# A gated mix of attention and feed-forward: both parts of an output tile in one PSUM bank for three of four query blocks, with the gate ratio folded into the softmax reciprocals

## The chip, the cores and the metric

The kernel runs on one core of one Trainium2 chip. The metric is the device time of one execution in microseconds (us). Engine names in the profile: PE is TensorE, PEld its weight loads, ACT is ScalarE, DVE is VectorE, POOL is GpSimd, SP is SyncE, whose queue issues most of the transfers.

## What is computed

For 2048 rows of width 512 the kernel computes attention with 32 heads of 16, a SwiGLU feed-forward part of width 1792, and a mix of both with one gate per row. All tensors are bf16.

```python
x = A_x
g = _sigmoid((x * gate_w).sum(-1, keepdims=True))
qkv = (x @ wqkv) ...                       # 32 heads of 16
p = _softmax(q @ k * 16 ** -0.5)           # 2048 keys
a = (p @ v) @ wo
b = (_silu(x @ w_gate) * (x @ w_up)) @ w_down
return g * a + (1 - g) * b
```

## The kernel before

**Units.** The queries are cut into four blocks of 512 (QB), the heads into eight groups of four (G). A unit is one block and one group: 32 units, ordered in UNIT (line 115): group 0 of all four blocks first, then groups 1 to 7 of block 0, of block 1, and so on. A unit has 16 key tiles of 128 keys, and each key tile four score blocks of 128x512, one for each head. A slot, the planner's clock, is one key tile: 512 slots.

**Two engines take exponentials.** PE writes the scores of two heads into one tile s_t of 128x1024 (emit_pair, line 715), of which there are two; ACT turns it into e_t (line 727). A key tile done so costs two ACT instructions. Other key tiles go to DVE (emit_d, line 748): PE writes each head's scores into a bank d_t, DVE evicts it to y_t with a scale that makes bf16 bits of an exponential, and once four are there, five more DVE operations on 128x2048 (z_t, u_t, two products, a last scale) improve them. Of these, the addition of the correction is an accumulating transfer on POOL's queue (line 795) or, near the end of the kernel, a DVE operation (add_here, line 786). v_unit (line 1368) decides when a tile goes to DVE: if by the planner's costs DVE would be done with it LEAD (16 us), or in the last unit LAST (11 us), before ACT is done.

**Weighted sums.** Four 32-column matmuls per key tile accumulate into one bank o_ps (pv, line 866). At the end of a unit DVE copies it to osb (post, line 903), and transfers on SP's queue put the head rows into onc and the denominators into a DRAM row dd (put, line 897).

**Softmax denominators.** At the end of a block, recip (line 928) loads the denominators back as 128x128 (dn), takes reciprocals on DVE (rn), stores them (rr), and loads them 16-fold as rows (rb). norm (line 944) multiplies onc by rb. The last two groups of the last block do this on chip (recip_here, and the end of the program).

**Feed-forward part.** For each block, 14 steps (gu_chain, line 650) make gate and up products of 128 of the 1792 columns in two banks gu; ACT takes a tanh (th), DVE makes gs and mt. The weights wg and wu come with w_load (line 642) on SP's queue, two steps ahead (line 1190). down_pieces (line 676) then multiplies mt by wd_t: 14 pieces of four 32-column matmuls into one bank dps for each of the four 128-row tiles of a block; DVE evicts it times the share 1 - g (omg) into bblk, or times ge = (1 - g) / g for the last block.

**Output.** For blocks 0 to 2, fin_pieces (line 997) multiplies onc by wo_t, four pieces into a bank a_ps; store (line 956) makes a_ps * g + bblk in one DVE operation and stores it. In the last block bblk is added by a matmul with ident (last_rows, line 966; last_pieces, tail), and the end of the program multiplies by g (lines 1503 to 1512).

**Gate.** gate_pieces and gate_end (lines 612 to 636): logits, clamped to -60 and 60, ge = exp(-logit), gval = 1 / (1 + ge) = g, omg = ge * gval = 1 - g.

**What sets the order.** The order of instructions on each engine is fixed when the program is built (ordered, line 146). A planner with a cost for each piece of PE, ACT and DVE work (spend, later, fill_dve) fills the gaps beside the scores. Side work is in chains with a release slot and a deadline (Pacer, line 48; lines 1170 to 1215); a chain that needs a bank takes one of three (m_tile, line 346), which it gives back when DVE has evicted it. The feed-forward part runs from slot 72 to slot 504, in the order of the blocks:

```python
FS = [(qb, fc) for qb in range(QB) for fc in range(FC)]                       # line 639
f0, f1 = 72, SLOTS - 8                                                        # line 1176
per = (f1 - f0) / QB
```

SP's queue issues its transfers in order, and a transfer that waits holds up those behind it. DRAM tiles such as dd and rr are in HBM.

Of the kernel before, what the change touches and what calls it, by code (L numbers as in the profile page):

```python
# [9 lines left out]
ALU = mybir.AluOpType  # L10
AX = mybir.AxisListType
BF16 = mybir.dt.bfloat16
F32 = mybir.dt.float32
# [66 lines left out]
def kernel(  # L80
# [13 lines left out]
    P = 128  # L94
    x = A_x.flatten_outer_dims()
    S, D = x.shape
    F = B_w_gate.shape[1]
    DH = 16
    H = D // DH
    G = H // 4  # L100
    NB = H // 8
    DC = D // P
    FC = F // P
    KT = S // P
    QBW = 512
    QB = S // QBW
    TQ = QBW // P
    assert H * DH == D and D % P == 0 and F % P == 0 and S % QBW == 0 and G == 8 and TQ == 4
    out_f = out.flatten_outer_dims()
# [3 lines left out]
    SLOTS = UNITS * KT  # L113
# [167 lines left out]
    gval = const.tile([P, KT], F32, name="gval")  # L281
    omg = const.tile([P, KT], F32, name="omg")
    ge = const.tile([P, KT], F32, name="ge")
    bblk = big.tile([P, TQ, D], BF16, name="bblk")


# [20 lines left out]
    def later(cost, f, ready=None, key=None):  # L307

        c = plan.chain
        if c is not None:  # L310
            c.owed += 1
        ready = plan.pe + 0.25 if ready is None else ready
        owed.insert(sum(o[0] <= ready for o in owed), (ready, cost, f, c, key))
# [101 lines left out]
    def columns(n, name, lhs, rhs, end, c0=0):  # L415

        st = {}

        def pc(k):
            def f():  # L420
                if k == 0:
                    st["p"] = m_tile(name)
                w, r = lhs(k), rhs(k)
                for j in range(4):
                    mm(st["p"][32 * j:32 * j + 32, c0:QBW], lhsT=w[:, 32 * j:32 * j + 32], rhs=r, start=(k == 0),
                       stop=(k == n - 1), tile_position=(0, 32 * j), skip_group_check=True)
                spend("C", 1)
                if k == n - 1:
                    end(st["p"])
            return f  # L430
        return [(1, pc(k), k == 0) for k in range(n)]
# [180 lines left out]
    def gate_pieces(t0):  # L612
        def f():
            gp = m_tile("glog")
            for t in (t0, t0 + 1):
                for dc in range(DC):
                    mm(gp[:, t:t + 1], lhsT=xT[:, dc, t * P:(t + 1) * P],
                       rhs=gw_col[:, dc:dc + 1], start=(dc == 0), stop=(dc == DC - 1))
            spend("F", 2)

            def end():
                vec.tensor_scalar(out=ge[:, t0:t0 + 2], in0=gp[:, t0:t0 + 2], scalar1=-60.0, scalar2=60.0,
                                  op0=ALU.max, op1=ALU.min)
                m_free(gp, plan.dve)
            later(0.15, end)
        return [(0.7, f, True, "F", None)]

    def gate_end():
        act(out=ge[:, :], in_=ge[:, :], func=ACT.Exp, scale=-1.0)
        plan.act += 0.2  # L630

        def end():
            vec.tensor_scalar(out=omg[:, :], in0=ge[:, :], scalar1=1.0, scalar2=None, op0=ALU.add)
            vec.reciprocal(gval[:, :], omg[:, :])
            vec.tensor_tensor(out=omg[:, :], in0=ge[:, :], in1=gval[:, :], op=ALU.mult)
        later(0.5, end, plan.act + 0.2)


    FS = [(qb, fc) for qb in range(QB) for fc in range(FC)]
    w_gate, w_up, gs_of = {}, {}, {}  # L640

    def w_load(i, gate):
# [33 lines left out]
    def down_pieces(qb, tq):  # L676

        def end(p):
            t, n = tq, qb * TQ + tq
            share = omg if qb < QB - 1 else ge  # L680
            vec.tensor_scalar(out=bblk[:, t, :], in0=p[:, 0:D], scalar1=share[:, n:n + 1],
                              scalar2=None, op0=ALU.mult)
            if qb == QB - 1:
                scaled.add(t)
            m_free(p, plan.dve)
        return columns(FC, "dps", lambda fc: mt[:, fc, tq * P:(tq + 1) * P], lambda fc: wd_t[:, fc, :],
                       lambda p: later(0.65, lambda: end(p)))
# [236 lines left out]
    def recip16(o, i):  # L924
        with nc.allow_low_precision(reason="bf16 reciprocal of softmax denominators is plenty accurate here"):
            vec.reciprocal(o, i)

    def recip(qb, g1, n0):

        n = 4 * g1  # L930
        dn = work.tile([P, P], BF16, tag="dn", name="dn")
        queue.dma_start(out=dn[0:4 * n, :], in_=dds[qb][0:n, :].rearrange("h (a c) -> (h a) c", c=P))

        def spread():
            rn = work.tile([P, P], BF16, tag="rn", name="rn")
            recip16(rn[0:4 * n, :], dn[0:4 * n, :])
            rr = dram.tile([H, QBW], BF16, tag="rr", name="rr")
            queue.dma_start(out=rr[0:n, :].rearrange("h (a c) -> (h a) c", c=P), in_=rn[0:4 * n, :])
            for b in range(g1 // 2):
                queue.dma_start(out=rb[:, b, :],  # L940
                                  in_=rr[8 * b:8 * b + 8, :].unsqueeze(1).broadcast_to([8, DH, QBW]))
        at.setdefault(n0 + 6, []).append(lambda: later(0.87, spread))
        for b in range(g1 // 2):
            def norm(b=b):
                vec.tensor_tensor(out=onc[qb][:, b, :], in0=onc[qb][:, b, :], in1=rb[:, b, :], op=ALU.mult)
                normed.add((qb, b))
            at.setdefault(n0 + 13 + b, []).append(lambda norm=norm: later(0.345, norm))

    def recip_here(osb):
# [2 lines left out]
        mm(dps[:, :], lhsT=sbc_t[:, :], rhs=osb[:, :], start=True, stop=True)  # L952
        rd = work.tile([P, QBW], BF16, tag="rd", name="rd")
        return dps, rd

    def store(t, a_ps, base, o_t=None):
        if o_t is None:
            o_t = opool.tile([P, D], BF16, tag="ot", name="o_t")[:, :]
        vec.scalar_tensor_tensor(out=o_t, in0=a_ps[:, 0:D], scalar=gval[:, t:t + 1], in1=base,
                                 op0=ALU.mult, op1=ALU.add)  # L960
        queue.dma_start(out=out_f[t * P:(t + 1) * P, :], in_=o_t)

    here_done = []
    a_ps = []
# [6 lines left out]
    def last_pieces():  # L971

        def keep(pa, pb):
            a_ps.extend([pa, pb])
        return two_banks(NB + 1, "a_l", last_rows(0), last_rows(1), keep, stop=False)
# [18 lines left out]
            w, r = last_rows(tq)(i)  # L994
            mm(a_ps[tq][:, 0:D], lhsT=w, rhs=r, start=(i == 0), stop=False)

    def fin_pieces(qb, tq):

        def end(p):
            store(qb * TQ + tq, p, bblk[:, tq, :])  # L1000
            m_free(p, plan.dve)
        return columns(NB, "a_ps", lambda b: onc[qb][:, b, tq * P:(tq + 1) * P], lambda b: wo_t[:, b, :],
                       lambda p: later(0.67, lambda: end(p)))

    kp0 = ps_s.tile([P, 2 * QBW], F32, tag="s", name="kp0")
    qp0 = m_tile("qp0")
# [164 lines left out]
    gates = [pace.add([(0.2, gate_end, False)], 40, 106, gates)]  # L1171

    prev = []
    fin_prev = []
    ffn = set()
    f0, f1 = 72, SLOTS - 8
    per = (f1 - f0) / QB
    for qb in range(QB):
        a0 = f0 + per * qb
        gus = []  # L1180
        for i in range(FC * qb, FC * qb + FC):
            gate_pcs, up_pcs = gu_chain(i)

            def first(f=gate_pcs[0][1], i=i):
                if i == 0:
                    w_load(0, True)
                    w_load(0, False)
                    w_load(1, True)
                    w_load(1, False)
                w_load(i + 2, True)  # L1190
                w_load(i + 2, False)
                f()
            for k, pcs in enumerate(([(1, first, True)] + gate_pcs[1:], up_pcs)):
                prev = [pace.add(pcs, 58, a0 + per * (0.6 if qb < QB - 1 else 0.68) * (i + 0.5 + k / 2 - FC * qb) / FC, begun=prev)]
                gus += prev
                ffn.update(prev)
        for tq in range(TQ):
            c = pace.add(down_pieces(qb, tq), 0 if qb else 100, a0 + per * (0.6 + 0.3 * (tq + 1) / TQ if qb < QB - 1 else 0.68 + 0.32 * (tq + 1) / TQ), (gus if tq == 0 else prev) + fin_prev + gates)
            prev = [c]
            ffn.add(c)  # L1200
        last = qb == QB - 1
        fin_prev = []
        if last:

            def ripe():
                return (all((qb, b) in normed for b in range(NB - 1)) and len(scaled) == TQ and here_done)
            pace.add(last_pieces(), SLOTS - KT // 2, SLOTS, prev, cond=ripe)
            break
        for tq in range(TQ):
            rel = (UNIT.index((qb, G - 1)) + 1) * KT + 24  # L1210
            dl = max(a0 + per * (0.9 + 0.1 * (tq + 1) / TQ), rel + 7 + 3 * tq)

            def cond(qb=qb):
                return all((qb, b) in normed for b in range(NB))
            fin_prev.append(pace.add(fin_pieces(qb, tq), rel, dl, prev + fin_prev, cond=cond))


    au = at_ = half = 0
# [134 lines left out]
        emit_pv(ns[0])  # L1353

    SLACK = 0.1
    LEAD, LAST = 16.0, 11.0
    TILE_US = 1.87

    def forward():
# [125 lines left out]
        mm(dt[:, 4 * tq:4 * tq + 4], lhsT=osb[:, tq * P:(tq + 1) * P], rhs=sel_t[:, :], start=True, stop=True)  # L1485
    rt = work.tile([P, 4 * TQ], BF16, tag="rt", name="rt")
    recip16(rt[:, :], dt[:, 0:4 * TQ])
    tail(3)
    rps = ps_s.tile([P, 2 * QBW], F32, tag="s", name="rps")
    for tq in range(TQ):  # L1490
        for j in range(4):
# [52 lines left out]
```

## Time and profile before

| what | value |
|---|---|
| time, median of 3 runs | 829.32 us (828.39 to 829.85) |
| the profiled execution's own time | 829.14 us |
| its span in the trace | 827.4 us |
| PE, DVE, ACT busy | 785.0, 794.5, 811.2 us |
| exponentials e_t on ACT | 844 |
| y tiles on DVE | 90 (360 evictions of d_t) |
| output operations on DVE for blocks 0 to 2 | 12 bblk, 12 o_t |
| first exponential starts, last one ends | 13.29 us, 819.05 us |
| gate's exponential on ACT | 178.9 us |

A group of the profile reads: line, engine, operation, written tile <- read tiles, shape, count, then busy time in all and mean ns of one, then the engine's idle time just before such instructions and what ended it. All DVE operations of the planner stand at line 170, all matmuls at 158, all ACT operations at 161, as these lines are helpers; they are told apart by their tiles. In a stage line the first number is the length of the stretch, then each engine's busy time with its count of instructions, PE's granted clock, the share of the DMA engines and GB/s. In the waits, each line is who waited for whom: us in total, times, longest.

### The profile page before, as it was taken

How to read it: one execution, taken by the hardware profiler on the slowest of the kernel's cores; microseconds unless marked ns; L12 is line 12 of the kernel's file. 1: busy time of each engine (PE TensorE's matmuls, PEld its weight loads, DVE VectorE, ACT ScalarE, POOL GpSimd, SP SyncE). 2: the span in 40 equal slices, each digit the busy share in tenths (PEclk: the TensorE clock that was granted, in tenths of full speed). 3: DMA queues.
4: the chain of work that ended last, by engine and by line, in shares of the span. 5: the costliest groups of instructions: out<-in, count | busy, mean ns of one | idle time of the engine just before them, and what ended most of it. 6: DMA issues, size and time to landing. Idle time of an engine off the chain costs nothing. (4 is left out here: it accounts for less than half of the span.)

```text
span 827.4 us, 20393 instructions
## 1 busy us (share of the span) xinstructions
PE 785.0 (95%) x8115; PEld 232.9 (28%) x8116; DVE 794.5 (96%) x1174; ACT 811.2 (98%) x913; POOL 102.3 (12%) x124
## 2 busy tenths in 40 slices
PE   8999999999999999999999999999998999999996
PEld 3322332322222222222222222222222222222222
DVE  6899999999999999999999999999999999999994
ACT  6999999999999999999999999999999999999996
POOL 5010111100001101101111100101111101111100
PEclk9999999999999999999999999999999999999999
DMA  8044346675544445654435474544435455453333
GB/s 178 11 77 90 59 91 119 126 158 99 107 91 84 96 85 119 118 119 87 82 71 100 81 152 84 119 94 89 80 69 105 87 114 111 103 101 69 75 66 77
DMA packets 100631, 79.54 MB, mean 96 GB/s; under 512 B 75680, under 2 KB 88568, under 8 KB 100536
## 3 DMA queue, kind: packets, MB, share of 16 engines
q0 software_dynamic: 12960, 47.19, 30.8%
q1 hardware_dynamic: 85848, 30.73, 16.0%
q8 instruction: 63, 1.03, 0.5%
q10 hardware_dynamic: 1728, 0.33, 0.2%
q14 instruction: 32, 0.26, 0.1%
HBM read 21.36 MB, written 2.34 MB: 29 GB/s over the span
## 5 line engine op out<-in xcount | busy, mean ns | idle before, releaser
L161 ACT ACTIVATE e_t<-s_t 128x1024 bf16<-128x1024 f32 x844 | 787.6, 1110 | 2.3 <-PE s_t L158 2.1
L158 PE MATMUL s_t<-qx,kaug 64*128 64x512 bf16 x1336 | 274.1, 383 | 24.4 <-ACT e_t L161 21.1
L170 DVE TENSOR_SCALAR y_t<-d_t 128x512 uint16<-128x512 f32 x360 | 234.1, 680 | 1.3 <-PE d_t L158 0.9
L158 PEld LDWEIGHTS <-kaug 64*128 64x128 bf16 x2048 | 111.7, 93 | 338.9 <-issue 329.2
L158 PE MATMUL o_ps<-e_t,vaug 128*32 128x512 bf16 x1688 | 168.1, 390 | 0.3 <-DVE osb L170 0.3
L158 PE MATMUL d_t<-qx,kaug 64*128 64x512 bf16 x296 | 102.0, 379 | 2.3 <-DVE y_t L170 1.4
L795 POOL DMA_DIRECT2D y_t<-u_t x45 | 44.5, 989 | 362.1 <-PE s_t L158 179.0
L158 PEld LDWEIGHTS <-vaug 128*32 128x32 bf16 (+1 forms) x2060 | 50.7, 93 | 123.0 <-issue 122.0
L158 PE MATMUL gu<-xT,wg 128*32 128x512 bf16 x896 | 76.8, 383 | 0.0
L158 PE MATMUL dps<-wd_t,mt 128*32 128x512 bf16 x896 | 76.1, 383 | 0.1
L795 POOL DMA_DIRECT2D y_t<-kaug x39 | 40.5, 1039 | 283.6 <-DVE kaug L170 108.1
L158 PE MATMUL gu<-xT,wu 128*32 128x512 bf16 x896 | 73.4, 382 | 0.1
L170 DVE TENSOR_SCALAR y_t<-y_t 128x2048 uint16<-128x2048 uint16 x90 | 61.5, 683 | 7.2 <-DMA y_t<-u_t 3.7
L170 DVE TENSOR_SCALAR z_t<-y_t 128x2048 uint16<-128x2048 uint16 x90 | 61.7, 686 | 1.0
L170 DVE TENSOR_TENSOR u_t<-u_t 128x2048 f16<-128x2048 f16 x45 | 55.0, 1221 | 0.9
L170 DVE TENSOR_TENSOR u_t<-u_t,z_t 128x2048 f16<-128x2048 f16 x45 | 54.6, 1214 | 0.1
L170 DVE TENSOR_TENSOR kaug<-kaug 128x2048 f16<-128x2048 f16 x39 | 47.6, 1221 | 0.9
L158 PE MATMUL s_t<-q,kaug 64*128 64x512 bf16 x212 | 43.5, 383 | 4.7 <-ACT e_t L161 4.2
L170 DVE TENSOR_TENSOR kaug<-kaug,z_t 128x2048 f16<-128x2048 f16 x39 | 47.4, 1215 | 0.1
L170 DVE SCALAR_TENSOR_TENSOR mt<-gs,gu 128x512 bf16<-128x512 bf16 x56 | 38.2, 682 | 2.4
L161 ACT ACTIVATE th<-gu 128x512 bf16<-128x512 f32 x56 | 38.2, 682 | 0.0
L170 DVE SCALAR_TENSOR_TENSOR gs<-th,gu 128x512 bf16<-128x512 bf16 x56 | 37.8, 676 | 0.1
(139 smaller groups left out, 556.3 us busy)
## 6 DMA issues: line engine op xcount, KB each, us to landing
y_t<-u_t POOLq DMA_DIRECT2D x45, 512.0 KB, 5.0
y_t<-kaug POOLq DMA_DIRECT2D x39, 512.0 KB, 5.1
wg<-in_B_w_gate_dram SPq DMA_DIRECT2D x56, 128.0 KB
wu<-in_B_w_up_dram SPq DMA_DIRECT2D x56, 128.0 KB
y_t<-wd_t POOLq DMA_DIRECT2D x6, 512.0 KB, 4.9
on<-osb SPq DMA_DIRECT2D x120, 16.0 KB
rb<-rr SPq DMA_DIRECT2D x15, 128.0 KB
wd_t<-in_B_w_down_dram SPq DMA_DIRECT2D x7, 256.0 KB
```

What stands on the lines that cost most here:

```text
L158: return ordered(nc.tensor.matmul(*args, **kw))
L161: ordered(nc.scalar.activation(*args, **kw))
L170: return lambda *a, **kw: ordered(f(*a, **kw))
L795: nc.gpsimd.dma_start(out=ya, in_=ua, accum_op=ALU.add)
```

## The change

The mix is written as (1 - g) * (b + g/(1 - g) * a). For blocks 0 to 2 the ratio g/(1 - g) = 1/ge, called odds, is multiplied into the reciprocals of the softmax denominators, so that onc carries it. Then the attention part and the feed-forward part of an output tile accumulate in one bank, ops, of 4 + 14 pieces (out_pieces), and one DVE operation times omg makes the output tile. fin_pieces, store and the evictions to bblk go for these blocks. The last block keeps its own way.

The odds are wanted as a row for each query, while the gate has them as a column, so twelve transfers of 128 elements each, one per 128-row tile, write them to DRAM, two slots apart after the gate's end, and recip loads them for 32 heads beside dn.

The feed-forward part of the last block is done first, then those of blocks 0, 1 and 2, since an output tile of these now needs the block's attention. The chains' release slots and deadlines follow. The gate's clamp is 40 instead of 60, LAST is 8.5 instead of 11, and one of the matmuls at the end is issued later.

```diff
+    odds = const.tile([P, KT], F32, name="odds")
+    odds_rows = []
...
-                vec.tensor_scalar(out=ge[:, t0:t0 + 2], in0=gp[:, t0:t0 + 2], scalar1=-60.0, scalar2=60.0,
+                vec.tensor_scalar(out=ge[:, t0:t0 + 2], in0=gp[:, t0:t0 + 2], scalar1=-40.0, scalar2=40.0,
...
+            vec.reciprocal(odds[:, :], ge[:, :])
+            odds_rows.append(dram.tile([KT, P], F32, tag="odds", name="odds_d"))
+
+            def turn_odds(t):
+                queue.dma_start(out=odds_rows[0][t:t + 1, :].rearrange("t p -> p t"), in_=odds[:, t:t + 1])
+            for t in range(TQ * (QB - 1)):
+                at.setdefault(plan.slot + 2 + 2 * t, []).append(lambda t=t: turn_odds(t))
...
-    FS = [(qb, fc) for qb in range(QB) for fc in range(FC)]
+    ORDER = [QB - 1] + list(range(QB - 1))
+    FS = [(qb, fc) for qb in ORDER for fc in range(FC)]
...
-            share = omg if qb < QB - 1 else ge
-            vec.tensor_scalar(out=bblk[:, t, :], in0=p[:, 0:D], scalar1=share[:, n:n + 1],
+            vec.tensor_scalar(out=bblk[:, t, :], in0=p[:, 0:D], scalar1=ge[:, n:n + 1],
                               scalar2=None, op0=ALU.mult)
-            if qb == QB - 1:
-                scaled.add(t)
+            scaled.add(t)
...
+        full = qb < QB - 1
+        if full:
+            rd = work.tile([P, QBW], BF16, tag="rd", name="rd")[:, :].bitcast(F32)
+            queue.dma_start(out=rd[:, 0:P], in_=odds_rows[0][TQ * qb:TQ * (qb + 1), :].unsqueeze(0).broadcast_to([H, TQ, P]))
...
-            recip16(rn[0:4 * n, :], dn[0:4 * n, :])
+            if full:
+                vec.reciprocal(rd[:, P:2 * P], dn[:, :])
+                vec.tensor_tensor(out=rn[:, :], in0=rd[:, P:2 * P], in1=rd[:, 0:P], op=ALU.mult)
+            else:
+                recip16(rn[0:4 * n, :], dn[0:4 * n, :])
...
-    def fin_pieces(qb, tq):
+    def out_pieces(qb, tq):
 
         def end(p):
-            store(qb * TQ + tq, p, bblk[:, tq, :])
+            t = qb * TQ + tq
+            o_t = opool.tile([P, D], BF16, tag="ot", name="o_t")
+            vec.tensor_scalar(out=o_t[:, :], in0=p[:, 0:D], scalar1=omg[:, t:t + 1], scalar2=None, op0=ALU.mult)
             m_free(p, plan.dve)
-        return columns(NB, "a_ps", lambda b: onc[qb][:, b, tq * P:(tq + 1) * P], lambda b: wo_t[:, b, :],
-                       lambda p: later(0.67, lambda: end(p)))
+            queue.dma_start(out=out_f[t * P:(t + 1) * P, :], in_=o_t[:, :])
+        cs = slice(tq * P, (tq + 1) * P)
+        return columns(NB + FC, "ops", lambda k: onc[qb][:, k, cs] if k < NB else mt[:, k - NB, cs],
+                       lambda k: wo_t[:, k, :] if k < NB else wd_t[:, k - NB, :], lambda p: later(0.65, lambda: end(p)))
...
+            rel = 100 if pos == 0 else (UNIT.index((qb, G - 1)) + 1) * KT + 16
+            c = pace.add((out_pieces if pos else down_pieces)(qb, tq), rel, a0 + per * (0.64 + 0.36 * (tq + 1) / TQ),
+                         (gus if tq == 0 else prev) + gates, cond=cond)
...
-    LEAD, LAST = 16.0, 11.0
+    LEAD, LAST = 16.0, 8.5
...
-    tail(3)
+    tail(2)
     rps = ps_s.tile([P, 2 * QBW], F32, tag="s", name="rps")
```

More of the change, by code (lines that the diff above doesn't have):

```diff
@@ L941, in spread @@
                                   in_=rr[8 * b:8 * b + 8, :].unsqueeze(1).broadcast_to([8, DH, QBW]))
-        at.setdefault(n0 + 6, []).append(lambda: later(0.87, spread))
+        at.setdefault(n0 + 6, []).append(lambda: later(1.1 if full else 0.87, spread))
         for b in range(g1 // 2):
@@ L954, in recip_here @@
         return dps, rd
[L956 to L961, printed above, removed]
     here_done = []
@@ L1173 @@
     prev = []
-    fin_prev = []
     ffn = set()
@@ L1177 @@
     per = (f1 - f0) / QB
-    for qb in range(QB):
-        a0 = f0 + per * qb
+    for pos, qb in enumerate(ORDER):
+        a0 = f0 + per * pos
         gus = []
-        for i in range(FC * qb, FC * qb + FC):
+        for i in range(FC * pos, FC * pos + FC):
             gate_pcs, up_pcs = gu_chain(i)
@@ L1193 @@
             for k, pcs in enumerate(([(1, first, True)] + gate_pcs[1:], up_pcs)):
-                prev = [pace.add(pcs, 58, a0 + per * (0.6 if qb < QB - 1 else 0.68) * (i + 0.5 + k / 2 - FC * qb) / FC, begun=prev)]
+                prev = [pace.add(pcs, 58, a0 + per * 0.64 * (i + 0.5 + k / 2 - FC * pos) / FC, begun=prev)]
                 gus += prev
@@ L1197, with cond, ripe @@
         for tq in range(TQ):
-            c = pace.add(down_pieces(qb, tq), 0 if qb else 100, a0 + per * (0.6 + 0.3 * (tq + 1) / TQ if qb < QB - 1 else 0.68 + 0.32 * (tq + 1) / TQ), (gus if tq == 0 else prev) + fin_prev + gates)
+            def cond(qb=qb):
+                return qb == QB - 1 or all((qb, b) in normed for b in range(NB))
+            rel = 100 if pos == 0 else (UNIT.index((qb, G - 1)) + 1) * KT + 16
+            c = pace.add((out_pieces if pos else down_pieces)(qb, tq), rel, a0 + per * (0.64 + 0.36 * (tq + 1) / TQ),
+                         (gus if tq == 0 else prev) + gates, cond=cond)
             prev = [c]
             ffn.add(c)
[L1201 to L1215, printed above, removed]
+            if pos == 0:
+                downs = prev
+    def ripe():
+        return (all((QB - 1, b) in normed for b in range(NB - 1)) and len(scaled) == TQ and here_done)
+    pace.add(last_pieces(), SLOTS - KT // 2, SLOTS, downs, cond=ripe)
     au = at_ = half = 0
```

## The prediction

> **What bounds the kernel now.** I read the page's busy table first, then the costliest groups kept apart by shape, then the busy times by stage (stretches of 40 us), then who waited for whom, and last the end of the timeline.
>
> ```profile
> PE 785.0 (95%) x8115; PEld 232.9 (28%) x8116; DVE 794.5 (96%) x1174; ACT 811.2 (98%) x913; POOL 102.3 (12%) x124
> ...
> L161 ACT ACTIVATE e_t<-s_t 128x1024 bf16<-128x1024 f32 x844 | 787.6, 1110 | 2.3 <-PE s_t L158 2.1
> ```
>
> Three engines look full, so shares alone do not name the bound. The second line does: over 844 exponentials ScalarE (ACT) was idle for 2.3 us in all. Between the first exponential (13.29 us in the timeline) and the end of the last (819.05 us) ACT has practically no hole. The stages say the same, and how near the other two are:
>
> ```profile
> core 0: us, PE busy (x) PEld busy (x) DVE busy (x) ACT busy (x) POOL busy (x), PEclk, DMA share, GB/s
> ...
> 280.00:320.00 40.00, 38.35 (x403) 11.38 (x406) 39.35 (x57) 40.00 (x47) 4.67 (x5) 1.00 0.57 118
> ...
> 520.00:560.00 40.00, 37.51 (x390) 10.76 (x387) 39.79 (x57) 40.00 (x47) 4.42 (x5) 1.00 0.54 106
> ...
> 680.00:720.00 40.00, 37.06 (x374) 10.96 (x370) 39.59 (x57) 40.00 (x46) 5.15 (x5) 1.00 0.56 117
> ```
>
> Added up from 40 to 800 us: ACT idle 1.4 us, VectorE (DVE) 11.3 us, TensorE (PE) 31.3 us. ACT sets the pace, DVE has little room, PE some. The waits agree: the largest one of PE is for ACT.
>
> ```profile
> PE s_t L158 <- ACT e_t L161: 26.3, 86, 0.8
> ...
> DVE y_t L170 <- DMA y_t<-u_t: 3.7, 2, 3.4
> ...
> PE d_t L158 <- DVE y_t L170: 1.4, 4, 0.7
> ```
>
> Score tiles go to either engine: a key tile costs ACT two exponentials or DVE one y tile (90 of 512 tiles). So DVE time pays only as far as it lets the planner move a tile from ACT to DVE. One exponential takes less than its mean of 1110 ns, as neighbours overlap: the timeline has 21 in 19.45 us from 799.59, which is (19.45 - 1.11) / 20 = 0.917 us from start to start, and 7 in 6.52 us from 23.98, which is 0.90. I use 0.915, so a tile is worth 1.83 us of ACT.
>
> **What the Trainium skill says.** "VectorE: DVE Perf Modes", section on the perf-mode tier table: a PSUM operand in fp32 runs at one element per cycle; `tensor_tensor` reaches two per cycle in bf16 from SBUF. The trace agrees: an eviction of 128x512 from PSUM starts 0.60 to 0.66 us after the one before, a 16-bit product of 128x2048 takes 1.22 us. The same page, section on the TRN2 errata, gives an fp32 `tensor_tensor` (N+151)/0.96 ns. "DMA: Bandwidth & Descriptors", rules for kernel authors: a last dimension that is not contiguous becomes one descriptor per element. Each small transfer of the change is then 128 elements of 4 bytes. The trace has one relative, gw_col below, with 512 elements.
>
> **The change, part by part.** Durations are from these rows (the time from start to start is some 0.08 us less than the mean):
>
> ```profile
> L170 DVE SCALAR_TENSOR_TENSOR o_t<-a_ps,gval,bblk 128x512 bf16<-128x512 f32 x12 | 8.9, 744 | 0.0
> L170 DVE TENSOR_SCALAR bblk<-dps,omg 128x512 bf16<-128x512 f32 x12 | 8.9, 742 | 0.1
> ...
> L170 DVE RECIPROCAL rn<-dn 128x128 bf16<-128x128 bf16 x3 | 2.8, 942 | 0.0
> ```
>
> 1. Evictions. For three query blocks, 12 bblk and 12 o_t operations become 12 of one kind: 12 x 0.66 = 7.9 us off DVE. Block 3 keeps its four bblk evictions; they only come early.
> 2. Ratio. Three bf16 reciprocals become three with an fp32 result. The same elements go through; the fp32-input one at the end (rd) takes 0.949, so 0 extra. Three fp32 products of 128x128 are new: 0.225 (bf16 sibling osb,rd) to 0.29 (the page's formula, an estimate); I take 0.29, 0.9 us. The reciprocal of 128x16 is 0.25 (gval's own). The clamp at 40 instead of 60 changes a constant only. Together +1.1.
> 3. So DVE is freed of 6.8 us. A y tile costs it 4 x 0.60 (evictions) + 0.60 + 0.66 + 1.13 + 1.13 + 0.60 = 6.5 us when its addition is a POOL transfer. The instruction order of the changed program, which I read without any time in it, has exactly one tile more: 91 y tiles, 842 exponentials. The new one is added by a DVE product-shaped instruction instead of a transfer. No row shows that operation; its nearest (u_t,z_t, mixed 16-bit types) says 1.15 to 1.22, the page's one-per-cycle price 2.29. I take 1.2. DVE: -6.8 + 7.7 = +0.9, at most +2.0. That lies beside ACT, within its 11.3 us of holes; without them it would cost all of it.
> 4. ACT: 2 x 0.915 = **1.83 us less**, on the path. All other ACT work is the same.
> 5. PE: the same output matmuls, in one accumulation of 18 pieces instead of 14 and 4. Four lone d_t scores replace two pairs, and eight small fillers come in: under 2 us, also if the 20-odd more switches between row and column pieces in the order cost 0.1 each (+2 us more). PE's 31 us hide it. A bank is held 18 pieces at once instead of 14 and then 4, but two of three stay free for the others; cost 0, or below nothing by the turnovers saved.
> 6. SP's queue. Twelve stores, two slots (some 3.2 us) apart from about 182 us, and three loads of rd:
>
> ```profile
> L170 SPq DMA_DIRECT2D gw_col<-in_gate_w_dram x1: 1222/1222/1222, 61.6 to 61.6; - x1
> ...
> L170 SPq DMA_DIRECT2D dd<-osb x30: 520/538/2022, 140.6 to 774.0; - x30
> ```
>
> A store of 128 elements lies between dd's 0.53 and gw_col's 1.22 us of issue; I take 0.6, so 7 us over some 40. Behind them in the queue are the weights wg and wu, which PE waits for, qx rows, and wd_t. The queue is full from 197 to 213 us and then has holes. A weight load is issued two feed-forward steps ahead, some 15 us, which covers it: 0 (up to 12 x 1.22 = 15 us of queue, still about covered). An rd load of 0.5 us rides beside dn, read six slots later. The longer reciprocal step adds 0.3 us before the rb loads; from rn (303.69) to the first use of rb (317.21) there are 13.5 us, of which the issues end by about 310.4. So 0; uncovered it would be 0.3 us three times.
> 7. Order. Block 3's feed-forward part goes first. At the end the last output tile is that of block 2: an eviction and a store off the path. a_l no longer waits for bblk.
> 8. The end. The last exponential is followed by 8.4 us of fixed work, nearly unchanged:
>
> ```profile
> 817.37 0.69 DVE L170 TENSOR_SCALAR y_t<-y_t 128x2048 uint16<-128x2048 uint16 x1 [3.45 <-DMA y_t<-u_t]
> ...
> 819.66 0.60 ACT L161 ACTIVATE osb<-o_ps 128x512 bf16<-128x512 f32 x1 [0.61 <-PE o_ps L158]
> 820.60 0.26 DVE L170 RECIPROCAL rt<-dt 128x16 bf16<-128x16 f32 x1 [2.54 <-PE dt L158]
> ```
>
> DVE idles here for a transfer; the new tile fills such holes. From the copy of the last-but-one osb DVE still has, in the new order, about 19 us of work by these rows; ACT has 22 exponentials, 22 x 0.915 + 1.1 = 21.2 us. DVE ends about 2 us ahead (1 us if the addition is slow), so the end stays ACT's. One al_o matmul (0.2) moves behind rps: 0 to -0.2, I take -0.1.
>
> **Sum.** The profiled execution was 829.14 us, span 827.4 and 1.74 around it. 829.14 - 1.83 - 0.1 = 827.2. The median of the runs stands 0.18 above that execution: **827.4**.
>
> **The rivals.**
> A. The gain is given back in waits. The new order puts d_t and s_t scores elsewhere; with DVE fuller PE may wait longer for a bank, and in order behind it stand the s_t that ACT needs. For it: DVE's holes shrink from 11.3 to about 9. Against: ACT lost only 2.3 us so in 806. If that doubles: 827.4 + 2.3 = 829.7; half of it 828.5. Centre 829.0.
> B. Slower: the stores block SP's queue. Place: 182 to 225 us, where wg and wu stand behind them. Price: only if one store holds the queue for more than about 2.5 us (12 x 2.5 = 30 us against the 15 us lead and the holes) do weights come late, by 5 us or more; PE then stalls in order, ACT is empty after the two score buffers. 827.4 + 5 = 832.4. For it: element-sized stores are the worst kind, and dd has a 2.0 us maximum. Against: gw_col, four times the elements, took 1.22.
> C. The change does more: fewer bank turnovers take away the 2.3 us as well: 825.1. PE waits for DVE's bank releases only 1.4 us now, so little speaks for it.
> D. It does nothing: excluded for the count, since two exponentials are gone from the program; only their place on the path could fail, which is A.
>
> **Chances.** Forecast 0.55, A 0.29, B 0.10, C 0.06. The forecast's own range is 826.6 to 828.3: runs of before spread 828.39 to 829.85, and waits of ACT may move by half a microsecond. About 0.2%, 1.66 us, is what a measurement tells from no change; the bound lies at 827.66, close above my point. Of the forecast 0.44 falls under it, with C 0.50. Its rest, 0.11, and A less 0.02 make the same 0.38; B with 0.02 of A is slower, 0.12. The range to hold 8 in 10 reaches into C and over most of A: 825.8 to 830.0.
>
> **What would show it.** In the changed profile: e_t x842, its idle still near 2 us, ACT again without holes from 40 to 800 us; y_t evictions x364; bblk x4 and o_t x12; the last exponential about 1.8 us earlier; the 8.4 us after it kept; odds stores of 0.5 to 1.2 us. I would be wrong if idle before e_t goes above 4 us (A; its releaser tells which wait), if wg or wu are waited for around 180 to 230 us (B), or if the last y_t ends after the last exponential.

## The result, and the profile after

The changed kernel took 853.72 us (median of 4 runs, 848.92 to 859.22) against 829.59 us for the kernel before beside it: ratio 1.0294, interval 1.0228 to 1.036. It is slower by 24 us where 2 us less was forecast. Its profiled execution took 855.17 us, span 853.5 us. Two executions in a slower state are left out of all ratios: one of the kernel before (849.13 us), and one of e12_changed_one_store below (1248.98 us), on which the profile of that run fell, which is therefore not read.

The busy table and the exponentials, which answer to those of before:

```profile
PE 795.5 (93%) x8123; PEld 232.3 (27%) x8124; DVE 797.4 (93%) x1176; ACT 811.2 (95%) x911; POOL 104.0 (12%) x124
...
L161 ACT ACTIVATE e_t<-s_t 128x1024 bf16<-128x1024 f32 x842 | 787.2, 1111 | 27.2 <-PE s_t L158 20.5
```

The stages of 40 us, first two of the kernel before, then four of the changed one:

```profile
200.00:240.00 40.00, 39.39 (x426) 11.71 (x423) 39.45 (x57) 39.98 (x48) 4.31 (x5) 1.00 0.54 112
240.00:280.00 40.00, 39.38 (x415) 11.17 (x416) 39.63 (x58) 40.00 (x45) 4.96 (x5) 1.00 0.38 74
```

```profile
160.00:200.00 40.00, 38.91 (x406) 11.02 (x403) 38.14 (x58) 40.00 (x48) 3.44 (x4) 1.00 0.54 117
200.00:240.00 40.00, 27.02 (x225) 6.29 (x226) 23.64 (x34) 24.29 (x27) 3.08 (x3) 0.79 0.48 71
240.00:280.00 40.00, 34.09 (x323) 8.22 (x323) 30.60 (x43) 30.68 (x34) 2.89 (x3) 0.87 0.55 79
280.00:320.00 40.00, 38.82 (x408) 11.14 (x407) 39.73 (x57) 40.00 (x45) 5.82 (x6) 1.00 0.42 82
```

There are 842 exponentials, as forecast, and ACT's work is the same; but ACT idled 27.2 us in front of them, not 2.3. The stages say where: 40.00 - 24.29 = 15.7 us and 40.00 - 30.68 = 9.3 us between 200 and 280 us, 25 us in all, and next to nothing elsewhere. So a cause that lasts through the kernel (the single bank, the output operations) is unlikely. In these 80 us all compute engines idle together. From 200 to 240 us the bytes moved fall from 112 to 71 GB/s, though the DMA engines count as busy for 0.48 of the time (0.54 before); from 240 to 280 us the kernel before moves as little (74 against 79). The granted clock falls as well, to 0.79 and 0.87, while PE has gaps, and single matmuls are longer: o_ps<-y_t took up to 612 ns from 190 to 280 us, up to 392 ns in the kernel before. How much of the 25 us the lower clock adds was not separated.

Who waited for whom in the changed kernel from 185 to 280 us (us in total, times, longest):

```profile
ACT e_t L161 <- PE s_t L158: 19.0, 12, 9.1
DVE y_t L170 <- DMA y_t<-kaug: 12.5, 3, 9.0
PE o_ps L158 <- DVE y_t L170: 12.0, 3, 8.7
...
PEld L158 <- DMA wg<-in_B_w_gate_dram: 6.1, 2, 4.4
...
PE gu L158 <- DMA wg<-in_B_w_gate_dram: 5.3, 2, 4.2
```

Read from the bottom up: weights wg came late for PE, and the additions y_t<-kaug, which POOL's queue issues, came late for DVE, whose y_t PE then waited for. PE works in order, so the next scores s_t stood behind these waits, and ACT ran empty. The two transfers are on different queues. Their own lines, first the stores and then the additions begun from 190 to 280 us in the changed kernel; the last line is the additions of the kernel before:

```profile
L170 SPq DMA_DIRECT2D odds_d<-odds x12: 339/506/2454, 193.8 to 254.0; - x12
```

```profile
DMA to landing us min/median/max: 5.0/9.8/14.5
```

```profile
DMA to landing us min/median/max: 4.5/4.9/6.0
```

The stores stand from 193.8 to 254.0 us, in the damaged stretch. Most take little time to issue (median 0.51 us, the longest 2.45), but an addition of 512 KB beside them takes 9.8 us instead of 4.9. SP's queue also waits for the landing of the stores, five times, for 20.4 us in all:

```profile
SPq L170 <- DMA odds_d<-odds: 20.4, 5, 7.1
```

Why it waits is not shown. What stands behind is held up: the store at 211.80 us waited 7.1 us so, and wg and wu followed it at 212.24 and 212.73 us. The chain of waits in this stretch, cut to its longest pieces (start, us, what), names such transfers as its links:

```profile
215.13 9.92 DMA y_t<-u_t
...
238.94 10.83 DMA wg<-in_B_w_gate_dram
...
254.38 12.82 DMA y_t<-kaug
```

**Theory.** The twelve stores stop the DMA engines that all queues share. **Rivals:** the new order of work with the single bank; twelve more transfers in SP's queue, whatever their shape; stores that hold up only what stands behind them in SP's queue, as in rival B of the prediction.

### The profile page after: what moved, and what is told of

It is laid out like the page before. It is cut to its first block, busy times and chain, and to the rows that moved or that the text cites. A ratio compares the mean times of both kernels' runs of the same rounds, so it can differ in the third digit from the quotient of the medians.

```text
span 853.5 us, 20406 instructions
## 1 busy us (share of the span) xinstructions
PE 795.5 (93%) x8123; PEld 232.3 (27%) x8124; DVE 797.4 (93%) x1176; ACT 811.2 (95%) x911; POOL 104.0 (12%) x124
## 3 DMA queue, kind: packets, MB, share of 16 engines
q1 hardware_dynamic: 88008, 30.93, 15.7%
q10 hardware_dynamic: 1728, 0.33, 0.2%
## 4 chain that ended last, share of the span: by engine, by line
DVE 35%; PE 20%; ACT 9%; DMA 6%; issue 5%; SPq 0%; DVEq 0%; ACTq 0%; POOLq 0%
DVE y_t L170 12%; ACT e_t L161 8%; PE s_t L158 7%; DVE kaug L170 7%; DVE u_t L170 6%; PE o_ps L158 4%; DVE z_t L170 3%; PE ops L158 3%; PE d_t L158 2%; DVE mt L170 2%; DMA y_t<-u_t 2%; PE gu L158 2%; DVE gs L170 2%; DMA y_t<-kaug 2%; DMA wg<-in_B_w_gate_dram 1%
## 5 line engine op out<-in xcount | busy, mean ns | idle before, releaser
L161 ACT ACTIVATE e_t<-s_t 128x1024 bf16<-128x1024 f32 x842 | 787.2, 1111 | 27.2 <-PE s_t L158 20.5
L158 PE MATMUL s_t<-qx,kaug 64*128 64x512 bf16 x1344 | 280.2, 387 | 23.4 <-ACT e_t L161 20.3
L170 DVE TENSOR_SCALAR y_t<-d_t 128x512 uint16<-128x512 f32 x364 | 237.2, 682 | 7.4 <-PE d_t L158 7.0
L158 PE MATMUL d_t<-qx,kaug 64*128 64x512 bf16 x288 | 100.2, 387 | 1.7 <-DVE y_t L170 0.4
L803 POOL DMA_DIRECT2D y_t<-u_t x45 | 48.6, 1081 | 366.6 <-PE s_t L158 210.8
L158 PE MATMUL gu<-xT,wg 128*32 128x512 bf16 x896 | 79.1, 394 | 6.2 <-DMA wg<-in_B_w_gate_dram 5.3
L803 POOL DMA_DIRECT2D y_t<-kaug x39 | 38.1, 977 | 300.6 <-PE s_t L158 125.2
L158 PE MATMUL ops<-wd_t,mt 128*32 128x512 bf16 x672 | 56.3, 383 | 0.0
L158 PE MATMUL o_ps<-y_t,vaug 128*32 128x512 bf16 x364 | 36.8, 391 | 12.5 <-DVE y_t L170 12.5
L158 PE MATMUL s_t<-q,kaug 64*128 64x512 bf16 x200 | 40.2, 384 | 3.6 <-ACT e_t L161 2.8
```

The source lines that it names most:

```text
L158: return ordered(nc.tensor.matmul(*args, **kw))
L161: ordered(nc.scalar.activation(*args, **kw))
L170: return lambda *a, **kw: ordered(f(*a, **kw))
L803: nc.gpsimd.dma_start(out=ya, in_=ua, accum_op=ALU.add)
```

## The experiments

**e1_stores_alone.** The kernel before, plus the reciprocal and the stores into a tile that nothing reads:

```diff
+            vec.reciprocal(odds[:, :], ge[:, :])
+            odds_rows.append(dram.tile([KT, P], F32, tag="odds", name="odds_d"))
+                queue.dma_start(out=odds_rows[0][t:t + 1, :].rearrange("t p -> p t"), in_=odds[:, t:t + 1])
```

> The kernel before with only the reciprocal of ge and the twelve element-sized stores added, to a DRAM tile that nothing reads. If the stores alone cost the time (theory S): 850 to 857 us, with the transfers y_t<-u_t and y_t<-kaug landing in 10 us or more between 200 and 270 us. If the new order of work or the single bank costs it (theory O): 829 to 830.5 us. If half and half: about 840.

849.37 us, ratio 1.0245 (1.0214 to 1.0276): 20.0 us by the stores alone, 829.41 beside it. Its waits from 190 to 290 us:

```profile
ACT e_t L161 <- PE s_t L158: 18.5, 10, 10.1
...
PE gu L158 <- DMA wg<-in_B_w_gate_dram: 9.4, 1, 9.4
```

With the whole rest of the change away, most of the loss is there. The additions landed in up to 11.8 us; their median (6.1) rose less than I expected; PE's longest wait for a transfer was for wg here.

**e2_row_stores.** The changed kernel, the source of each store replaced:

```diff
-                queue.dma_start(out=odds_rows[0][t:t + 1, :].rearrange("t p -> p t"), in_=odds[:, t:t + 1])
+                queue.dma_start(out=odds_rows[0][t:t + 1, :], in_=wo_t[8 * t:8 * t + 1, 0, 0:2 * P].bitcast(F32))
```

> The changed kernel with the twelve stores kept in number, place, queue and bytes (512 each), but each reads one contiguous row of another tile in one partition, so the ratio that it loads is not the gate's (that part of the computation is changed). If it is the elements of 4 bytes that cost (S): 827 to 828.5 us, two exponentials under the kernel before. If it is twelve more transfers on SP's queue and its waits, whatever their shape (theory Q): 850 or more. O: about 853.

The rows that it stores are of another tile, so its output is not the mix. 829.33 us, ratio 0.9994 (0.9986 to 1.0002). Twelve transfers in the same places cost nothing once they are whole rows. The rivals of order and of the number of transfers fall. The gain over before that was expected is not seen; see below.

**e3_turn_on_pe.** The changed kernel without element-sized stores:

```diff
+        mm(p[0:KT, 0:P], lhsT=odds[:, :], rhs=ident[:, :], start=True, stop=True)
...
+            vec.tensor_copy(out=odds_t, in_=p[0:KT, 0:P])
...
+            queue.dma_start(out=odds_rows[0][:, :], in_=odds_t)
```

> The changed kernel with the ratio as bf16, turned by one matmul with ident into a bank, copied, and stored by one transfer of 16 rows of 512 bytes. S: 827 to 828.5 us. O: about 853. Q: 828 to 830, since eleven transfers are gone too.

828.57 us against 829.41, ratio 0.9989 (0.9981 to 0.9997): the only version whose interval lies wholly under the kernel before, by 0.1%. Its exponentials:

```profile
L161 ACT ACTIVATE e_t<-s_t 128x1024 bf16<-128x1024 f32 x842 | 786.0, 1099 | 1.5 <-PE s_t L158 0.9
```

**e4_stores_apart.** Seven slots between the stores instead of two:

```diff
-                at.setdefault(plan.slot + 2 + 2 * t, []).append(lambda t=t: turn_odds(t))
+                at.setdefault(plan.slot + 2 + 7 * t, []).append(lambda t=t: turn_odds(t))
```

> The changed kernel with the twelve stores seven slots apart instead of two (some 11 us instead of 3). If each store stops the DMA engines for a while of its own (S, cost per store): the loss stays mostly, 845 us or more, spread over 180 to 310 us. If only their crowding costs, as one waits for the other: 828 to 833 us. O: about 853.

866.33 us, ratio 1.0439 (1.0418 to 1.0459): 36.9 us, worse than close together, 36.9 / 12 = 3.1 us each. Crowding is not the cause. That each store meets other transfers anew when they are spread out would explain the rise; it is argued, not shown. The waits of this run:

```profile
ACT e_t L161 <- PE s_t L158: 39.3, 19, 7.2
DVE y_t L170 <- DMA y_t<-kaug: 28.2, 7, 8.4
PE o_ps L158 <- DVE y_t L170: 27.5, 6, 6.7
```

From 180 to 360 us PE waited only 1.1 us for wg. So most of this loss comes through the additions of POOL's queue, in which no such store stands. A hold-up in SP's queue alone does not account for it.

The next four, and e9, change the shape of the stores in the kernel before (e1's edit; shortened here, 12 stands for TQ * (QB - 1)):

```diff
+ e5: out=odds_rows[0][t, :, 0:1]          # rows of 512 bytes, one element in each
+ e6: out=odds_s[:, t:t + 1]               # to a column in SBUF
+ e7: out=odds_rows[0][0:12, :].rearrange("t p -> p t"), in_=odds[:, 0:12]   # one transfer
+ e8: out=odds_rows[0][t, :, :], in_=odds[:, :]    # 64 bytes from each partition
+ e9: out=odds_rows[0][t, :, 0:1]          # rows of 64 bytes, one element in each
```

> The kernel before with the twelve element-sized stores alone, as in the run with the stores alone, but each of the 128 elements of a store goes to a row of DRAM of its own, 512 bytes from the next. If neighbouring elements in one stretch of 512 bytes hold each other up (theory L, one line): 829 to 832 us. If any write of 4 bytes to DRAM costs (theory W): 846 to 852 us.

829.72 us, ratio 1.0002 (0.9992 to 1.0012). No cost.

> The same twelve transfers of 128 elements of 4 bytes, but from a column of one SBUF tile to a column of another, not to DRAM. If the cost lies in the writes to DRAM (L or W): 829 to 831 us. If it lies in reading single elements or in the number of descriptors (theory D): 846 to 852 us.

829.11 us, ratio 0.9999 (0.9990 to 1.0008). No cost.

> The kernel before with one store of all twelve columns, 1536 elements of 4 bytes to twelve stretches of 512 bytes, in place of twelve stores. If each element costs (L and W alike): 840 to 850 us, or somewhat less, where twelve stretches take writes side by side. If each transfer costs a fixed time: 830 to 832 us.

832.38 us, ratio 1.0036 (1.0022 to 1.0049): 3.3 us for the same 1536 elements to the same addresses.

> The kernel before with twelve stores of all sixteen columns as they lie, 128 pieces of 64 bytes to 8 KB of DRAM without gaps: sixteen times the bytes, the same number of pieces. L or W, if only pieces below 64 bytes are bad: 829 to 831 us. If all pieces under 512 bytes that share a stretch are bad: 845 us or more.

829.23 us, ratio 1.0003 (0.9993 to 1.0013). No cost.

> The kernel before with the twelve element-sized stores, the elements 64 bytes apart in DRAM: eight share a stretch of 512 bytes, none a stretch of 64. If the stretch within which writes hold each other up is 64 bytes or less: 829 to 831 us. If it is 512 bytes: some 845 to 850 us.

829.38 us, ratio 1.0007 (1.0000 to 1.0014): at most about 1 us.

Here is one stage, 220 to 240 us, with the stores close together (e1) and then with the elements 512 bytes apart (e5):

```profile
220.00:240.00 20.00, 10.60 (x72) 2.01 (x64) 7.77 (x11) 7.72 (x10) 0.00 (x0) 0.62 0.76 53
```

```profile
220.00:240.00 20.00, 19.68 (x217) 5.88 (x215) 19.86 (x30) 20.00 (x25) 2.54 (x3) 1.00 0.53 110
```

The same count of transfers, elements and bytes, and of packets over the whole kernel (102359 in each). With neighbours the DMA engines count as 76% busy and move 53 GB/s; with gaps, 53% and 110 GB/s, and ACT is full. So neither 4-byte elements (e5, e9), nor the number of descriptors (e6), nor small pieces in DRAM (e8) cost more than some 1 us here. What costs is many 4-byte writes that follow each other into neighbouring places of DRAM. In e7 the same addresses are written, but consecutive elements go to twelve rows in turn, which fits the small loss; that the order makes it is argued, not shown.

**e10_on_acts_queue.** The costly stores of e1, issued from ACT:

```diff
-                queue.dma_start(out=odds_rows[0][t:t + 1, :].rearrange("t p -> p t"), in_=odds[:, t:t + 1])
+                nc.scalar.dma_start(out=odds_rows[0][t:t + 1, :].rearrange("t p -> p t"), in_=odds[:, t:t + 1])
```

> The kernel before with the twelve neighbouring-element stores issued from ACT's queue, so that nothing stands behind them in SP's. If the stores stop the DMA engines that all queues share (theory E): still 845 us or more, with y_t additions and wg landing late. If only the transfers behind them in SP's queue suffer (theory Q, rival B of the prediction): 829 to 834 us, a few of them for the issue on ACT.

844.28 us, ratio 1.0185 (1.0163 to 1.0208): 15.4 us, just under the 845 us of theory E. Its waits:

```profile
ACT e_t L161 <- DMA qx<-qst: 4.1, 1, 4.1
PE gu L158 <- DMA wg<-in_B_w_gate_dram: 4.1, 2, 2.6
ACT e_t L161 <- DMA odds_d<-odds: 3.4, 1, 3.4
...
ACT e_t L161 <- DMA qx<-bq: 1.5, 1, 1.5
```

wg in SP's queue is still late, though no such store stands in front of it: the stop reaches other queues. The additions of POOL's queue landed in up to 9.7 us (190 to 280 us). But 3.4 us and perhaps 5.6 more are ACT's own waits for transfers, so this run gives no clean share for either.

**e11_pe_turn_lead_12.** e3 with tiles sent to DVE later:

```diff
-    LEAD, LAST = 16.0, 8.5
+    LEAD, LAST = 12.0, 8.5
```

> The kernel with the ratio turned by PE, and LEAD 12 instead of 16 us, which gives 840 exponentials instead of 842. If ACT is the bound and each exponential is worth 0.915 us: 826.7 us, 1.8 under the run with 842. If tiles planned so late make PE wait for y_t: 829 or more.

849.03 us, ratio 1.0246 (1.0232 to 1.0261). Two exponentials fewer than e3, and 20 us lost:

```profile
ACT e_t L161 <- PE s_t L158: 20.6, 19, 5.3
...
PE o_ps L158 <- DVE y_t L170: 9.4, 5, 4.1
PE o_ps L158 <- DVE osb L170: 6.1, 8, 1.5
```

PE waited 15.5 us for DVE, and ACT for PE. So here two exponentials fewer brought nothing, as DVE was not done in time.

**e12_changed_one_store.** The changed kernel with e7's one store:

> The changed kernel with its twelve stores as one store of twelve columns, all else kept. If costs add up: 828.6 (ratio turned by PE) plus 3.2 (one store alone, over before), 831 to 832.5 us. If the change loses by something else too: over 835.

840.10 us in the median of the three executions that count (840.63 of all four), ratio 1.0141 (1.0125 to 1.0157): some 8 us more than the sum of 831 to 832.5. The next four runs take this up.

**e13_single_column** (e1 with `range(1)`) and **e14_stores_of_32** (e1 with `in_=odds[0:32, t:t + 1]`):

> The kernel before with one of the twelve stores: one column, 128 neighbouring elements. If each store has a price of its own (20.0 / 12 = 1.7 us, or 3.1 as with the stores far apart): 830.5 to 832 us. If one store is hidden by the slack of transfers and only a row of them runs it out: 829 us.

829.07 us, ratio 0.9999 (0.9990 to 1.0008). One addition still landed in 10.7 us (175 to 280 us), and nothing was lost: the slack of the transfers hid it.

> The kernel before with twelve stores of 32 neighbouring elements instead of 128. If the stop goes with the number of elements in a 64-byte stretch times the stretches (four times fewer in all): up to 834 us. If each store has a fixed price: 845 us or more.

832.70 us, ratio 1.0049 (1.0033 to 1.0066): 3.7 us for a quarter of the elements, against 20.0. That fits a cost by the element (20.0 / 4 = 5.0, less what slack hides), and not one by the store.

**e15_changed_one_store_again**, and **e16_one_store_later**, the same kernel with

```diff
-                at.setdefault(plan.slot + 2 + 2 * t, []).append(lambda t=t: turn_odds(t))
+                at.setdefault(plan.slot + 40, []).append(lambda t=t: turn_odds(t))
```

> The changed kernel with one store of twelve columns once more, for an undisturbed profile. About 840 us as before; the loss should stand right behind the store, at 194 to 215 us, with ACT waiting for PE and PE for wg, wu or a y_t addition. If it stands elsewhere, the change loses by something else.

839.12 us, ratio 1.0123 (1.0108 to 1.0138). The store is issued at 193.82 us. Waits of this run from 180 to 240 us:

```profile
ACT e_t L161 <- PE s_t L158: 8.9, 3, 7.1
DVE y_t L170 <- DMA y_t<-kaug: 8.0, 1, 8.0
PE o_ps L158 <- DVE y_t L170: 7.7, 1, 7.7
```

One addition landed in 13.5 us, DVE waited 8.0 us for it, PE 7.7 for DVE, ACT 7.1 at a stretch for PE: a single late transfer makes most of the 10 us.

> The changed kernel with its one store of twelve columns at another place, 38 slots later, behind transfers of on and ahead of q rows that are wanted later. If the place in the queue makes the price: 829 to 833 us. If the price is the store's own in this order of work: 838 to 842 us.

830.81 us, ratio 1.0021 (1.0011 to 1.0032). The same store at 254.4 us costs 2 to 3 us over e3 (by the ratios to before, 1.0021 and 0.9989). So the price hangs on where in the order the store stands, and e12's surplus needs no other fault of the change.

## Why the prediction was wrong, point by point

- **Steps 1 to 3 (DVE's account) held.** 842 exponentials, 364 evictions. DVE's busy time in e3 is 795.6 us, 1.1 more than before; I had 0.9, and e3 adds a copy of 0.27. The sizes, by shape, in the changed kernel:

```profile
L170 DVE TENSOR_SCALAR o_t<-ops,omg 128x512 bf16<-128x512 f32 x12 | 8.9, 741 | 0.0
...
L170 DVE RECIPROCAL rd<-dn 128x128 f32<-128x128 bf16 x3 | 2.8, 945 | 0.0
...
L170 DVE TENSOR_TENSOR y_t<-y_t,kaug 128x2048 uint16<-128x2048 uint16 x1 | 1.2, 1224 | 0.0
...
L170 DVE TENSOR_TENSOR rn<-rd 128x128 bf16<-128x128 f32 x3 | 0.9, 292 | 0.1
```

  The fp32 product takes 0.292 us where I took 0.29, the addition 1.22 for 1.2, the reciprocal the same as in bf16.
- **Step 4 (1.83 us off ACT) was partly right.** Without the stores, e3 shows 0.84 us (its interval reaches from 0.2 to 1.6 us), and e2 none that is clear. In e3's own profile, which fell on the fastest of its 20 executions (826.98 us), the stretch from the first exponential (12.88 us) to the end of the last (816.62) is 803.7 us, 2.0 less than before; but its ACT waits were only 1.1 us, e2's 2.7. Waits of that size come and go between kernels, as rival A had it on a small scale. Where the other 1 us goes is not settled.
- **Steps 5, 7 and 8 held.** In e3 the single bank and the new order cost nothing beyond the 1 us left open. In e3 the last y_t ends at 813.65 us, 3 us before the last exponential; I had 2.
- **Step 6 failed**, where it puts the stores at 0: "A store of 128 elements lies between dd's 0.53 and gw_col's 1.22 us of issue; I take 0.6", covered by the weights' lead. The issue was sized well at the median (0.51 us), though the longest took 2.45 us, and the stores stood from 193.8 to 254.0 us, not within some 40 us from 182. But issue was not what the stores cost. The step left out that SP's queue waits for their landing (20.4 us in the changed kernel) and that transfers on other queues land late beside them (up to 14.5 us instead of 6.0). I took gw_col as the relative that bounds them from above; it reads single elements from DRAM, while the stores write them, neighbour by neighbour. No row that I had read wrote single elements to DRAM, and I should have left the upper end open. e1 prices the step at 20.0 us instead of 0.
- **Rival B** had the outcome, the place and the victims (wg from 182 us on), with 0.10 of the chance. Its mechanism is a part of the loss at most. SP's queue did stand for the stores, for up to 7.1 us at a time in the changed kernel and 7.1 us in all in e1. But in e4, the costliest version, PE waited 1.1 us for a weight, and e10 lost 15.4 us with no such store in SP's queue. POOL's additions were late too, which B did not count, and the price was 24 us, not 3 over before.
- The cover that I named for the weights, a 15 us lead, was real for one store (e13: no cost). Twelve used it up: in e1 PE waited 9.4 us for wg. The additions, for which the planner allows 6 us, have slack that differs: one that landed in 10.7 us cost nothing in e13, one of 13.5 us cost DVE 8.0 us in e15.
- What the Trainium skill says ("DMA: Bandwidth & Descriptors", rules for kernel authors), that a last dimension which is not contiguous lowers to one descriptor per element, fits the stores: e1 has 102359 packets, 1728 more than before for 1536 elements. But the number of descriptors is not the cost: e5, e6 and e9 have as many packets and lose next to nothing.

## What to carry to other kernels

A tiny transfer can delay transfers on other queues (here POOL's and SP's); what it costs is read from the landing times of the others beside it, not from its own issue. Before a column is written to DRAM as a row, element by element, turn it on chip (one matmul with an identity, 0.22 us here, and a copy of 0.27 us) and store whole rows. And when a bound for a new operation is taken from a relative in the profile, check that it is the same in direction, in target and in spacing, or leave the upper end open.

## What the runs showed of the hardware that was not expected

- Writes of 4 bytes to neighbouring DRAM addresses, 128 to a transfer, twelve transfers: 20.0 us. The same elements 64 or 512 bytes apart in DRAM, or written to SBUF, or 64-byte pieces without gaps: at most some 1 us. Why neighbouring writes cost so much stays open, and distances between 4 and 64 bytes were not tried.
- The delay of the additions has two forms in the packet records of the traces. A packet stands: the longest of 4096 bytes on POOL's queue from 175 to 360 us took 6.5 us in the changed kernel and 6.1 us in e1, against 0.7 us before and 0.8 us in e5. Or the first packet comes late: 9.1 us after the issue in e15 (at 196.8 us), against 1.4 us for the addition at 195.9 us in e3. Which part of the way from issue to landing holds them is not shown.
- Spreading such stores over time made them dearer (36.9 us instead of 24); why is argued above, not shown.
- The same store of 1536 elements cost 3.3 us in the kernel before, and 10 or 2 to 3 us in the changed one, by where in the order it stood.
